# Score maxima in two parts, a batch's logits copied out at once, and unit transposes between the first maxima

## The chip, the cores and the metric

One core of a Trainium2 chip runs the kernel. The metric is the time of one execution in microseconds (us), taken on the device; several executions give a median. The engines are TensorE (PE; its weight loads are PEld), VectorE (DVE), ScalarE (ACT), GpSimd (POOL) and SyncE (SP), which here only issues transfers.

## The reference, cut to what matters

Three stages follow one another; the change touches the first and its hand-over to the second.

```python
def _attn_ref(q, k, v):                      # 4 batches, 8 heads, 1152 rows, 64 columns
    q_pool = q.reshape(B, H, S // 2, 2, D).mean(axis=3)
    scores = scale * np.matmul(q_pool, k.transpose(0, 1, 3, 2))
    scores = scores - np.max(scores, axis=-1, keepdims=True)
    attn = np.exp(scores)
    attn = attn / (np.sum(attn, axis=-1, keepdims=True) + 1e-09)
    return np.matmul(attn, v)

def _moe_ref(x, phi, w1, w2):                # 2304 tokens, 512 wide, 8 experts with 4 slots
    logits = x @ phi
    d = np.exp(logits - logits.max(0, keepdims=True))
    d /= d.sum(0, keepdims=True) + 1e-09
    slot_input = d.T @ x
    ...                                      # an expert's two layers on its slots
    c = np.exp(logits - logits.max(1, keepdims=True))
    c /= c.sum(1, keepdims=True) + 1e-09
    return c @ slot_out
...                                          # then a second, routed mixture of experts
```

## The kernel before

Two heads of one batch form a pair, and there are 16 pairs. A pair is worked off in 18 steps (`NCH`), numbered `s` = 0 to 17, by `step(n)` with `n = 18 * i + s`: the first nine steps take one half of the queries, the other nine the other half, and each step one block of 128 keys. In a step TensorE multiplies queries and keys for both heads (`scores`: lines 374 and 375; the second product adds, as a 65th row, the negated row maximum), and ScalarE takes the exponential out of PSUM (line 376). In step 10 the products with v of the pair's first half follow, 36 matmuls in a row (`weighted`, line 433), and those of its second half in step 1 of the next pair.

The row maxima that `scores` needs have to be known a pair ahead. `s_max(i, j)` computes one of nine blocks of 128 rows: three matmuls of 384 keys each (line 334) into one PSUM tile `s` of three banks, and one VectorE reduction over all 1152 columns (line 343). The pool `ps_s` holds one such tile, so that the next `s_max` starts when that reduction is over. With `apart=True`, used twice at the start, the three parts go into three tiles of the other pool (`new_e`, five banks) and get a reduction each (line 340). `n_group` transposes five or four finished maxima (line 349), ScalarE copies them, and SyncE's queue carries them to the 65th row (line 354).

What else stands in a step is set by tables at the top of the file, from step number to action: `MAXS` (which maximum), `SIDE` (the small groups: q transposes `q0`, `q1`, maxima `n0`, `n1`, row sums `r`, outputs `x0` to `x2`), `BATCH` (m, d, s: the work that follows a batch's last pair, steps above 17 counting into the next pair), `TURN`, `HIGH`, `REST` (transposing and splitting keys of a later pair), `HEADS` (carrying split keys into the tiles `u`, lines 291 and 292), `LOADW` (weights of the second stage), `KLOAD` (keys from HBM, line 246). The first pair has tables of its own (`FIRST`, `FMAX`, `FTURN`). Each engine and each transfer queue works in the order in which the code emits; an instruction that waits holds up all behind it on its engine or queue. All transfers here but the first few stand in SyncE's one queue.

`max_group(b)` transposes a finished batch's logits into a tile of `ps_s`; VectorE takes their maximum, `smax`, from there, and ScalarE then the exponential into `dt`. `d_group` transposes `dt` back, and `sl_group` forms the slot sums. `warm(t, n)` is n transposes of the unit matrix whose results nobody reads.

## Time and profile before

| | |
|---|---|
| median of 3 runs | 701.2 us (697.88 to 702.91) |
| the profiled execution | 700.93 us, of which 698.9 us are the span of the trace |
| instructions | 12442 |
| busy share of the span | PE 94%, PEld 71%, DVE 56%, ACT 49%, POOL 53% |
| mean granted TensorE clock | 0.975 |

The page gives busy times of one execution, a strip of 40 slices of about 17.5 us each, and the chain of work that ended last. The first stage fills the span up to about 510 us, the second up to about 573 us, the rest is the third. In a row of the timeline the first number is the start, the second how long it took (or, with x3, how long three lasted from the first start to the last end), and a bracket at the end says how long the engine stood idle before and what ended that.

### The profile page before, as it was taken

What the parts mean: (1) busy time and instruction counts of PE and PEld (TensorE: products, weight loads), DVE (VectorE), ACT (ScalarE), POOL (GpSimd) and SP (SyncE); (2) the same over time, 40 slices, a digit from 0 to 9 for tenths busy, and PEclk for the clock granted to TensorE, in tenths of its full rate; (3) what the DMA queues carried; (4) which work ended last, traced back from release to release, by engine and by line L of the source; (5) the groups of instructions that cost most, each with busy time, mean ns of one, the idle gap of its engine ahead of it and who ended that gap; (6) DMA issues with size and microseconds to landing.
All of it is one profiled execution on the core that took longest, in us unless ns stands there. A gap on an engine that the chain in (4) does not pass through costs nothing.

```text
span 698.9 us, 12442 instructions
## 1 busy us (share of the span) xinstructions
PE 655.8 (94%) x4330; PEld 495.7 (71%) x4330; DVE 391.9 (56%) x611; ACT 341.7 (49%) x944; POOL 372.4 (53%) x403
## 2 busy tenths in 40 slices
PE   5788999999999999999999999999988989999996
PEld 3655788777687778768778876877753366888885
DVE  5456667667676666767657676764344325522210
ACT  2245566555566556546555654645514046632221
POOL 5454788688777878867678886767700001000000
PEclk9579999999999999999999999999999999999999
DMA  7958778897778978858897895844899924031111
GB/s 135 179 88 177 164 142 215 156 202 198 128 191 165 205 194 150 206 102 214 157 188 189 153 216 92 215 110 106 297 349 385 354 88 155 18 73 46 46 45 48
DMA packets 185090, 114.28 MB, mean 164 GB/s; under 512 B 120888, under 2 KB 158520, under 8 KB 185024
## 3 DMA queue, kind: packets, MB, share of 16 engines
q1 hardware_dynamic: 182976, 112.46, 67.7%
q10 hardware_dynamic: 2048, 0.98, 0.8%
q8 instruction: 36, 0.59, 0.4%
q14 instruction: 30, 0.25, 0.1%
HBM read 66.14 MB, written 4.72 MB: 101 GB/s over the span
## 4 chain that ended last, share of the span: by engine, by line
PE 73%; DVE 8%; DMA 5%; ACT 3%; issue 2%; POOL 1%; SPq 0%; ACTq 0%; POOLq 0%
PE e L433 20%; PE h L1150 14%; PE s L334 11%; PE e L374 8%; PE e L375 7%; DVE nm L343 6%; PE e L469 3%; DMA w<-in_moe_w 2%; DMA en<-in_moe_expert_emb 2%; PE e L410 1%; ACT pt L376 1%; PE e L302 1%; PE h L868 1%; PE h L842 1%; DMA x<-in_moe_w 1%
## 5 line engine op out<-in xcount | busy, mean ns | idle before, releaser
L343 DVE TENSOR_REDUCE nm<-s 128x1 f32<-128x1152 f32 x142 | 192.1, 1353 | 120.1 <-PE s L334 120.0
L376 ACT ACTIVATE pt<-e 128x288 f32<-128x288 f32 x576 | 199.4, 413 | 63.7 <-PE e L375 55.5
L391 POOL TENSOR_TENSOR acc<-acc,pt 128x576 f32<-128x576 f32 x127 | 180.0, 1418 | 15.0 <-ACT pt L376 9.0
L374 PE MATMUL e<-qh,u 128*128 128x288 f32 x576 | 180.1, 328 | 1.2 <-ACT pt L376 1.2
L375 PE MATMUL e<-ql,u 65*128 65x288 f32 x576 | 165.2, 303 | 2.8 <-DMA ql<-nr 2.8
L433 PE MATMUL e<-pt,v 128*64 128x288 f32 x1152 | 149.7, 415 | 0.0
L334 PE MATMUL s<-kh,qb 128*128 128x384 f32 x426 | 109.4, 366 | 15.7 <-DVE nm L343 8.7
L433 PEld LDWEIGHTS e<-pt,v 128*64 128x64 f32 x1152 | 81.0, 139 | 59.6 <-ACT pt L376 5.4
L374 PEld LDWEIGHTS e<-qh,u 128*128 128x128 f32 x576 | 111.9, 194 | 13.6 <-issue 7.6
L375 PEld LDWEIGHTS e<-ql,u 65*128 65x128 f32 x576 | 112.0, 194 | 4.1 <-DMA u<-kh 2.2
L334 PEld LDWEIGHTS s<-kh,qb 128*128 128x128 f32 x426 | 72.1, 197 | 27.9 <-DVE nm L343 17.9
L435 ACT ACTIVATE xu<-e 128x288 f32<-128x288 f32 x32 | 13.1, 410 | 128.5 <-PE e L433 128.5
L389 POOL TENSOR_TENSOR acc<-pt 128x576 f32<-128x576 f32 x32 | 45.4, 1418 | 53.5 <-PE e L418 45.1
L394 DVE TENSOR_REDUCE part<-pt 128x576 f32<-128x1728 f32 x32 | 68.1, 2129 | 0.0
L397 POOL TENSOR_TENSOR acc<-acc,part 128x576 f32<-128x576 f32 x31 | 43.6, 1407 | 36.6 <-DVE part L394 36.5
L1150 PE MATMUL h<-xh,hh 128*128 128x512 f32 x144 | 57.5, 400 | 0.0
L1150 PE MATMUL h<-xh,hl 128*128 128x512 f32 x144 | 57.0, 396 | 0.0
L1150 PE MATMUL h<-xl,hh 128*128 128x512 f32 x144 | 57.0, 396 | 0.0
L285 POOL TENSOR_TENSOR kl<-kl,kh 128x384 fp32r<-128x384 f32 x48 | 48.0, 1001 | 0.6 <-ACT kh L281 0.6
L1127 POOL CAST xh<-x 128x512 fp32r<-128x512 f32 x6 | 3.4, 613 | 63.8 <-PE t L1110 63.8
L1142 DVE SCALAR_TENSOR_TENSOR hl<-c,hh 128x512 fp32r<-128x512 f32 (+1 forms) x22 | 14.0, 642 | 37.8 <-ACT hh L1141 37.8
L469 PE MATMUL e<-ip,xu 128*128 128x192 f32 x160 | 33.9, 328 | 0.0
(232 smaller groups left out, 686.5 us busy)
## 6 DMA issues: line engine op xcount, KB each, us to landing
w<-in_moe_w SPq DMA_DIRECT2D x23, 1024.0 KB
u<-kh SPq DMA_DIRECT2D x96, 192.0 KB
kn<-in_k SPq DMA_DIRECT2D x64, 144.0 KB
u<-kl SPq DMA_DIRECT2D x96, 96.0 KB
v<-in_v SPq DMA_DIRECT2D x32, 288.0 KB
w<-in_moe_w SPq DMA_DIRECT2D x36, 256.0 KB
qh<-hq SPq DMA_DIRECT2D x60, 144.0 KB
qr<-in_q SPq DMA_DIRECT2D x28, 160.0 KB
```

The costliest lines, as they stand in the source:

```text
L285: eng.tensor_tensor(out=t, in0=t.bitcast(F32), in1=hi, op=ALU.subtract)
L334: nc.tensor.matmul(ss[c], qb[j // 6][:, j % 6, :], kh[i % 2][:, c * KC : (c + 1) * KC], start=True, stop=True)
L343: nc.vector.tensor_reduce(out=nm, in_=s[:, :, 0:KC], axis=AX.XY, op=ALU.max, negate=True)
L374: nc.tensor.matmul(e, us[j // 3][:, h, ks], qh[:, h, qs], start=True, stop=False)
L375: nc.tensor.matmul(e, ws[j // 3][:, h, ks], ql[:, h, qs], start=False, stop=True)
L376: nc.scalar.activation(out=pt(n)[:, h, :], in_=e, func=AF.Exp, scale=1.0 / 16.0)
L389: eng.tensor_tensor(out=acc, in0=pt(n - 1), in1=pt(n), op=ALU.add)
L391: eng.tensor_tensor(out=acc, in0=acc, in1=pt(n), op=ALU.add)
L394: nc.vector.tensor_reduce(out=p["part"], in_=pts[n // 3].rearrange("p j h q -> p h q j"), axis=AX.X, op=ALU.add)
L433: nc.tensor.matmul(p["pv"][own[h], 0:HQ], vs[:, h, j, :], pt(n)[:, h, :], start=j == 0, stop=j == J - 1)
L469: nc.tensor.matmul(t[:, n * PW : (n + 1) * PW], xu[:, m * P : (m + 1) * P], ip[:, hp, :], start=True, stop=True)
L1150: nc.tensor.matmul(o, x[:, c, sl], y[:, c, :], start=c + r == 0, stop=c == FC - 1 and r == 2)
```

## The change

- `s_max` without `apart` uses two tiles in place of one: `sa` of two banks for the first two parts and `sb` of one bank for the third, with a reduction each, so that two numbers remain for a block (`nm` becomes 5 x 2). After the last block of a group one more reduction takes the lesser of each two (`nn`), and `n_group` transposes that. With `apart`, the last small step is the lesser of two numbers by `tensor_tensor`.
- `max_group` uses a bank of the five, and ScalarE copies the logits to `dt` at once; maximum and exponential are then taken from `dt`. `sl_group` of the last batch uses `sb`.
- Tables: the maximum of block 3 in step 9 (was 8); m, d, s of a batch at 19, 20, 21 (was 18, 19, 21); the first turned part of the keys in step 0 (was 2), in the first pair one part in step 8 (was 9); the second part of `HEADS` in step 16 (was 15), behind the `KLOAD` of step 15; the first weights of a pair in step 1 (was 3).
- Five groups of unit transposes (24, 6, 12, 16 and 18) stand between and behind the first pair's first five maxima.

```diff
--- before.py
+++ after.py
@@ -32,14 +32,14 @@
 
 
 SIDE = {5: 'q1', 7: 'r', 9: 'x0', 1: 'q0', 13: 'x2', 12: 'n0', 3: 'n1', 14: 'x1'}
-MAXS = {2: 0, 4: 1, 6: 2, 8: 3, 10: 4, 16: 7, 1: 8, 14: 6, 11: 5}
-BATCH = {18: 'm', 19: 'd', 21: 's'}
-
-TURN = {2: 0, 9: 2, 12: 1}
-FTURN = {9: 1, 11: 0, 10: 2}
+MAXS = {2: 0, 4: 1, 6: 2, 10: 4, 16: 7, 1: 8, 14: 6, 11: 5, 9: 3}
+BATCH = {21: 's', 20: 'd', 19: 'm'}
+
+TURN = {9: 2, 12: 1, 0: 0}
+FTURN = {11: 0, 10: 2, 8: 1}
 HIGH = {16: 2, 13: 1, 11: 0}
 REST = {17: 0, 8: 1, 10: 2}
-HEADS = (11, 15, 17)
+HEADS = (11, 16, 17)
 QHEADS = 6
 VISITS = (10, 19)
 
@@ -48,9 +48,11 @@
 FQHEADS = 14
 
 PREAT = 2
-LOADW = (3, 6, 10)
+LOADW = (1, 6, 10)
 QLOAD, KLOAD, VLOAD, QSUM = 5, 15, 6, 12
 FQLOAD, FQSUM = 12, 17
+
+NIDLE = (24, 6, 12, 16, 18)
 
 
 @with_exitstack
@@ -322,31 +324,41 @@
     def s_max(i, j, apart=False):
         p = pairs[i]
         if j in (0, 5):
-            p["nm", j] = sm.tile([P, 5], F32, tag="nm", name="nm", bufs=3)
+            p["nm", j] = sm.tile([P, 5, 2], F32, tag="nm", name="nm", bufs=3)
         j0 = 5 if j > 4 else 0
-        nm = p["nm", j0][:, j - j0 : j - j0 + 1]
+        nm = p["nm", j0][:, j - j0]
+
+        def part(t, c):
+            nc.tensor.matmul(
+                t[:, 0:KC], qb[j // 6][:, j % 6, :], kh[i % 2][:, c * KC : (c + 1) * KC], start=True, stop=True
+            )
+
         if apart:
-            ss = [new_e()[:, 0:KC] for _ in range(3)]
+            ts = [new_e() for _ in range(3)]
+            for c in range(3):
+                part(ts[c], c)
+            n1 = sm.tile([P, 1], F32, tag="n1", name="n1", bufs=2)
+            for t, n in zip(ts, (nm[:, 0:1], nm[:, 1:2], n1)):
+                nc.vector.tensor_reduce(out=n, in_=t[:, 0:KC], axis=AX.X, op=ALU.max, negate=True)
+            nc.vector.tensor_tensor(out=nm[:, 0:1], in0=nm[:, 0:1], in1=n1, op=ALU.min)
         else:
-            s = ps_s.tile([P, 3, 512], F32, tag="s", name="s")
-            ss = [s[:, c, 0:KC] for c in range(3)]
-        for c in range(3):
-            nc.tensor.matmul(
-                ss[c], qb[j // 6][:, j % 6, :], kh[i % 2][:, c * KC : (c + 1) * KC], start=True, stop=True
-            )
-        if apart:
-            n3 = sm.tile([P, 3], F32, tag="n3", name="n3", bufs=2)
-            for c in range(3):
-                nc.vector.tensor_reduce(out=n3[:, c : c + 1], in_=ss[c], axis=AX.X, op=ALU.max, negate=True)
-            nc.vector.tensor_reduce(out=nm, in_=n3, axis=AX.X, op=ALU.min)
-        else:
-            nc.vector.tensor_reduce(out=nm, in_=s[:, :, 0:KC], axis=AX.XY, op=ALU.max, negate=True)
+            s = ps_s.tile([P, 2, 512], F32, tag="sa", name="sa")
+            for c in range(2):
+                part(s[:, c], c)
+            nc.vector.tensor_reduce(out=nm[:, 0:1], in_=s[:, :, 0:KC], axis=AX.XY, op=ALU.max, negate=True)
+            s = ps_s.tile([P, 512], F32, tag="sb", name="sb")
+            part(s, 2)
+            nc.vector.tensor_reduce(out=nm[:, 1:2], in_=s[:, 0:KC], axis=AX.X, op=ALU.max, negate=True)
+        if j in (4, J - 1):
+            n = j - j0 + 1
+            nn = p["nn", j0] = sm.tile([P, 5], F32, tag="nn", name="nn", bufs=3)
+            nc.vector.tensor_reduce(out=nn[:, 0:n], in_=p["nm", j0][:, 0:n], axis=AX.X, op=ALU.min)
 
 
     def n_group(i, part):
         j0, n = (5, J - 5) if part else (0, 5)
         t = new_t()
-        nc.tensor.transpose(t[0:n, 0:P], pairs[i]["nm", j0][:, 0:n], ident)
+        nc.tensor.transpose(t[0:n, 0:P], pairs[i]["nn", j0][:, 0:n], ident)
         nr = sm.tile([5, P], F32R, tag="nr", name="nr", bufs=2)
         nc.scalar.activation(out=nr[0:n], in_=t[0:n, 0:P], func=AF.Copy)
         ql = sets[i % 2][2]
@@ -500,16 +512,18 @@
 
 
     def max_group(b):
-        t = ps_s.tile([P, 3, 512], F32, tag="s", name="s")[:, 0, :]
+        t = new_t()
         nc.tensor.transpose(t[:, 0:P], lk[:, b * JB : (b + 1) * JB, :].rearrange("p m n -> p (m n)"), ident)
         n = P + 64
         nc.tensor.transpose(t[:, P:n], xb[b]["l4"].rearrange("p m n -> p (m n)"), ident[0:64, 0:64])
+
+        dt = xb[b]["dt"] = xp.tile([P, n], F32, tag="dt", name="dt")
+        nc.scalar.activation(out=dt, in_=t[:, 0:n], func=AF.Copy)
         yield
-        nc.vector.tensor_reduce(out=smax[b], in_=t[:, 0:n], axis=AX.X, op=ALU.max, negate=True)
+        nc.vector.tensor_reduce(out=smax[b], in_=dt, axis=AX.X, op=ALU.max, negate=True)
         if b:
             nc.vector.tensor_tensor(out=smax[b], in0=smax[b], in1=smax[b - 1], op=ALU.min)
-        dt = xb[b]["dt"] = xp.tile([P, P + 64], F32, tag="dt", name="dt")
-        nc.scalar.activation(out=dt, in_=t[:, 0 : P + 64], func=AF.Exp, bias=smax[b])
+        nc.scalar.activation(out=dt, in_=dt, func=AF.Exp, bias=smax[b])
         if b:
             cor = xb[b]["cor"] = sm.tile([P, 1], F32, tag="cor", name="cor", bufs=1)
             nc.scalar.activation(out=cor, in_=smax[b - 1], func=AF.Exp, scale=-1.0, bias=smax[b])
@@ -550,7 +564,7 @@
             nc.tensor.matmul(t[ms, cs], d[0:64, 1, ms], xr[:, cs], start=False, stop=True, tile_position=(0, m * NS))
 
     def sl_group(b):
-        t = ps_s.tile([P, 3, 512], F32, tag="s", name="s")[:, 0, :] if b == B - 1 else new_t()
+        t = ps_s.tile([P, 512], F32, tag="sb", name="sb") if b == B - 1 else new_t()
         slot_sums(b, t)
         yield
         if b == B - 1:
@@ -608,16 +622,26 @@
         nc.gpsimd.memset(t[:, PQ:], 0.0)
     nc.gpsimd.memset(ip[:, :, P:PW], 0.0)
     nc.gpsimd.tensor_copy(ip[:, :, 0:P], ident.unsqueeze(1).to_broadcast([P, DC, P]))
+
+    idle = new_e()
+    warm(idle, NIDLE[0])
     s_max(0, 0)
     next(gq[1])
     s_max(0, 1, True)
     run_all(gq[1])
+    idle = new_e()
+    warm(idle, NIDLE[1])
     s_max(0, 2)
+    warm(idle, NIDLE[2])
     s_max(0, 3, True)
     s_max(0, 4)
+    idle = new_e()
+    warm(idle, NIDLE[3])
 
     load_qk(1, "q", nc.scalar)
     run_all(n_group(0, 0))
+    idle = new_e()
+    warm(idle, NIDLE[4])
     by_heads(0, 2)
     load_qk(1, "k")
     load_v(0)
```

## Rows read from the trace of the kernel before

**Rows 1.** The page's strip: granted TensorE clock in tenths, 40 slices.
```profile
PEclk9579999999999999999999999999999999999999
```

**Rows 2.** The page's chain of work that ended last, by line.
```profile
PE e L433 20%; PE h L1150 14%; PE s L334 11%; PE e L374 8%; PE e L375 7%; DVE nm L343 6%; PE e L469 3%; DMA w<-in_moe_w 2%; DMA en<-in_moe_expert_emb 2%; PE e L410 1%; ACT pt L376 1%; PE e L302 1%; PE h L868 1%; PE h L842 1%; DMA x<-in_moe_w 1%
```

**Rows 3.** Windows of two pairs each: length, busy us per engine, clock, DMA.
```profile
93.64:150.95 57.31, 56.66 (x417) 45.21 (x416) 40.17 (x53) 34.18 (x100) 45.52 (x47) 1.00 0.85 183
150.95:210.90 59.95, 58.93 (x435) 45.91 (x434) 41.87 (x60) 34.83 (x102) 46.16 (x45) 1.00 0.79 172
268.40:331.40 63.00, 60.72 (x435) 46.94 (x434) 43.38 (x61) 34.85 (x103) 46.18 (x45) 0.97 0.79 168
```

**Rows 4.** Timeline of TensorE, 99 to 107 us: around three maxima.
```profile
99.34 0.30 PE L375 MATMUL e<-ql,u 65*128 65x288 f32 x1
99.47 0.68 PE L334 MATMUL s<-kh,qb 128*128 128x384 f32 x3
100.00 0.29 PE L374 MATMUL e<-qh,u 128*128 128x288 f32 x1
...
101.04 0.29 PE L375 MATMUL e<-ql,u 65*128 65x288 f32 x1
101.61 0.79 PE L334 MATMUL s<-kh,qb 128*128 128x384 f32 x3 [0.28 <-DVE nm L343]
102.24 0.29 PE L374 MATMUL e<-qh,u 128*128 128x288 f32 x1
...
105.76 0.29 PE L375 MATMUL e<-ql,u 65*128 65x288 f32 x1
...
106.75 0.30 PE L374 MATMUL e<-qh,u 128*128 128x288 f32 x1
```

**Rows 5.** Groups by form on VectorE: busy us, mean ns, idle before.
```profile
L343 DVE TENSOR_REDUCE nm<-s 128x1 f32<-128x1152 f32 x142 | 192.1, 1353 | 120.1 <-PE s L334 120.0
L340 DVE TENSOR_REDUCE n<-e 128x1 f32<-128x384 f32 x6 | 3.0, 549 | 0.0
```

**Rows 6.** One line's instructions on VectorE: ns, min/median/max.
```profile
L510 DVE TENSOR_TENSOR smax<-smax,smax x3: 160/1216/1224, 297.2 to 514.4; 128x1 f32<-128x1 f32 x3
```

**Rows 7.** Timeline of TensorE and VectorE in the first 13 us.
```profile
1.37 3.03 PE L572 MATMUL e<-ident 128*128 128x128 f32 x13 [1.37 <-POOL ident masks.py:199]
8.34 0.90 PE L302 MATMUL e<-ident,qr 128*128 128x128 f32 x3 [3.94 <-DVE qr L259]
...
12.99 1.36 DVE L343 TENSOR_REDUCE nm<-s 128x1 f32<-128x1152 f32 x1 [1.01 <-PE s L334]
```

**Rows 8.** A window at the first stage's end, columns as in rows 3.
```profile
514.00:517.40 3.40, 3.40 (x16) 2.96 (x16) 1.35 (x6) 1.18 (x4) 0.00 (x0) 0.50 1.03 400
```

**Rows 9.** Timeline of SyncE and TensorE, first pair, maxima to the 65th row.
```profile
21.06 1.62 SPq L354 DMA_DIRECT2D ql<-nr  x2
...
37.92 1.36 SPq L354 DMA_DIRECT2D ql<-nr  x2
...
41.63 0.61 PE L375 MATMUL e<-ql,u 65*128 65x288 f32 x1 [0.24 <-DMA ql<-nr]
```

**Rows 10.** Timeline of SyncE, first pair, steps 11 to 17.
```profile
50.52 0.68 SPq L291 DMA_DIRECT2D u<-kh  x1
...
60.28 1.52 SPq L354 DMA_DIRECT2D ql<-nr  x2
```

**Rows 11.** Timeline of SyncE and VectorE: keys from HBM and their use.
```profile
39.38 2.83 SPq L246 DMA_DIRECT2D kn<-in_k  x4
...
46.48 0.58 DVE L278 STREAM_TRANSPOSE kl<-kn 128x384 f32<-128x384 f32 x1 [1.90 <-DMA kn<-in_k]
...
89.89 0.68 SPq L291 DMA_DIRECT2D u<-kh  x1
...
92.67 2.85 SPq L246 DMA_DIRECT2D kn<-in_k  x4
```

**Rows 12.** Timeline of SyncE and the chain, behind the last maxima.
```profile
490.45 26.56 SPq L127 DMA_DIRECT2D w<-in_moe_w  x12
...
545.11 14.40 DMA w<-in_moe_w
```

## The prediction

> **What bounds the kernel now.** I read the page first, then the chain of work that ended last, then windows of the granted clock, then TensorE's timeline pair by pair, and last VectorE's, ScalarE's and SyncE's timelines at the places where TensorE stood.
>
> The chain runs mostly over TensorE, but 6% of the span in it are the maximum reduction of line 343, right behind the 11% of the matmuls of line 334 that feed it [rows 2]. That reduction is not there because VectorE is full: over two ordinary pairs of 57.31 us TensorE is busy for 56.66, VectorE for 40.17, ScalarE for 34.18 [rows 3]. It is there because one tile of three banks serves all maxima, so that TensorE can't begin a block before the reduction of the block before has ended.
>
> What such a wait costs is read from TensorE's timeline [rows 4]. Between the last product of a step (line 375) and the next step's first (line 374) lies one block of maxima. Where it did not wait, the two starts are 99.34 and 100.00, 0.66 apart. At 101.04 and 102.24 they are 1.20 apart, and the block's row names the reduction: a loss of 0.54. At 105.76 and 106.75 they are 0.99 apart: a loss of 0.33. So 0.87 us of a pair of some 28.65 us are lost here, and the same two waits come back in each of the pairs 1 to 14, which compute nine blocks for the pair behind them: 14 x 0.87 = 12.2 us.
>
> Second, the ends of batches. The windows of two pairs around them last 59.95 us for the first batch and 63.00 us for the second (the third is like the second), against 57.31 [rows 3]. The first batch's excess, 2.64, bounds what the batch's own matmuls cost. The other two lose 63.00 - 59.95 = 3.05 us more each, 6.1 in all; their mean clock of 0.97 says that some 3.8 us ran at 1.2 GHz, which alone is 1.9 of the 3.05.
>
> Third, the start. The clock is low in parts of the first three slices [rows 1]. The first slice's digit is not to be trusted: 13 transposes there take 3.03 us, the last one's end included, so some 0.22 each [rows 7], the pace of a window whose clock reads 0.50 (16 transposes in 3.40 us, 0.213 each) [rows 8].
>
> **The change part by part.** The sum is made against the profiled execution, 700.9 us; the median of the runs is 701.2.
>
> *Maxima in two parts.* The trace has no reduction over 768 columns. It lies between 0.549 (384 columns) and 1.353 us (1152) [rows 5]; a straight line through both gives 0.951. Both ends of the wait move: the reduction that frees the next block's first tile starts one matmul earlier (three take 0.68 [rows 4], so about 0.17) and is 1.353 - 0.951 = 0.40 shorter. The tile is free about 0.57 earlier than now. Ahead of the longer wait TensorE stood from about 101.17 (0.13 behind the start at 101.04) to 101.61 [rows 4], that is 0.44. So both waits of a pair should go. The third part has its own bank, free 0.549 after the first reduction, before TensorE comes to it. VectorE pays 0.951 + 0.549 - 1.353 = 0.15 more a block, some 1.4 us a pair, and the small reduction once a group; in 28.65 us it is busy for about 20 [rows 3], so this lies beside TensorE's work. Moving block 3 a step later spreads the blocks and costs nothing by itself. Bounds: 0 (another engine stops TensorE at the same places) to 12.2. The candidate is ScalarE, whose exponentials come two a step; on average it has room (34.18 of 57.31), so I stay near the upper end and take **-11.0**.
>
> *A batch's logits.* They leave the maxima's tile, and ScalarE's copy frees their bank at once, so the maxima no longer wait through reduction, comparison and exponential. But the transposes of `dt` come in step 2, one step after those of the logits, and TensorE works in order: they wait for VectorE's queue (now with the turned keys ahead), for a comparison of two numbers that takes 1.22 us in those two batches and 0.16 us in the last one, where GpSimd is idle [rows 6, 8], and for the exponential. The 36 matmuls of step 1 cover most of that. Bounds 0 to 6.1; I take half, **-3.0**.
>
> The row shows the same instruction at 0.16 us where GpSimd was idle, and at 1.22 us where it was at work. The Trainium skill's "SBUF — State Buffer", section "SBUF: two separate sides", says why: a VectorE instruction with two SBUF inputs and GpSimd exclude each other from one pair of ports for whole instructions. It speaks against the change in one place: the lesser of two numbers with `apart` becomes such an instruction. By it the first maxima could wait for one GpSimd instruction twice more, at most about 2 x 1.06 us by this row, 2.1 us on the sum.
>
> *Unit transposes at the start.* The 24 stand behind the q transposes of 8.34 and ahead of the first maximum, whose reduction now starts at 12.99 [rows 7]. At 0.213 each (16 in 3.40 us) they last from about 8.98 to 14.1; at half that, an estimate for 2.4 GHz, to 11.55. Two matmuls of the first block follow, 0.5 us at full clock and 1.0 at half. So the first reduction starts at 15.1 in the worst case, 2.1 later than now, and in the best case 0.4 earlier, since it waits for two matmuls in place of three and the keys are late anyway. 13 and 16 transposes in rows 7 and 8 kept the slow pace for over 3 us, so I take a rise on the way: 1.0 later. The reductions behind stand back to back on VectorE and grow by three times 0.15 and one small one, 0.5: the first five maxima reach SyncE's queue at 22.6 in place of 21.06 [rows 9].
>
> In the window of rows 8 TensorE did nothing but unit and other transposes at 0.50, and the slot sums behind it ran at full pace, so transposes do raise the clock here. The Trainium skill, "TensorE: Matmul & The Clock Gate", section "Part 4: PE-mode transpose", says that the full clock doesn't engage for transposes. By that rule the 24 all run slowly, the delay is 2.1 in place of 1.0, and the sum comes to 688.7; the trace disagrees.
>
> What the higher clock could give from there to 41 us is not to be had. The second group's maxima go out at 37.92, and TensorE takes them at 41.63 [rows 9]; between 21.06 and 37.92 SyncE's queue issues 20 other transfers back to back and then stands for only some 0.3 us. A faster TensorE waits there for the queue, and idle it loses the clock again. So the delay stays: 1.5 - 0.3 = +1.2. In steps 11 to 17 the dense maxima of the first pair will stop waiting too, but the maxima for pair 1 again stand behind 14 transfers, issued from 50.52 to 60.28 with some 0.5 us of idle time [rows 10]. I count -0.5. Together **+0.7**; bounds -0.7 (best start) and +2.3 (worst start, nothing back).
>
> *Moved transfers.* With `HEADS` at 16, four transfers of split keys (2.6 us) stand behind the load of keys and not ahead of it, so that this load starts at about 89.9 in place of 92.67 [rows 11]. That pays for turning keys in step 0. The weights of step 1 go out while the 36 matmuls run. Zero, with a rival below.
>
> *The end.* `max_group` of the last batch gets one more ScalarE pass, some 0.4 us. TensorE later waits 14.40 us for weights whose loads start at 490.45 [rows 12], when the first stage gives memory back; the pass lies under that. As the loads move with the first stage, what it gains reaches the end. Zero.
>
> Sum: 700.9 - 11.0 - 3.0 + 0.7 = **687.6 us**.
>
> **The rivals.**
>
> *Late keys (slower).* VectorE now turns keys in step 0, ahead of the maximum of step 1, and stands there until the load is in. In the first pair a load issued at 39.38 was used at 46.48 after a wait, 7.1 us [rows 11]. From 89.9 this gives 97.0; the turn, two reductions and the split of q behind it take some 2.5, to 99.5, and TensorE needs the bank that this split frees at about 100.0 [rows 4]. Slack 0.5. Each further microsecond costs one in each of 13 pairs: at 8.6 us after issue the gain is gone, at 9.3 us the loss is 1.7 x 13 = 22, **709.7 us**. For it: transfers fill 0.85 of the time [rows 3]. Against: 7.1 was measured behind a load of v.
>
> *ScalarE takes over (no change by measurement).* Half the waits come back on the exponentials, a batch saves 0.75: 700.9 - 5.5 - 1.5 + 0.7 = **694.6 us**.
>
> *Everything goes (faster still).* Both waits and all of 6.1, the start at its lower bound: 700.9 - 12.2 - 6.1 - 0.7 = **681.9 us**.
>
> *The parts don't free the tile earlier.* If VectorE came late to the first reduction anyway, the two waits of a pair would stay and grow by 0.15 each: 700.9 + 14 x 2 x 0.15 + 0.7 = **705.8 us**. Against it: VectorE idled for 120 us in front of these reductions [rows 5].
>
> **How the numbers follow.** Forecast 0.55 (own range 684 to 692), everything goes 0.15, ScalarE 0.17, no earlier tile 0.05, late keys 0.08. The range 679 to 698 leaves out the last two and the edges of the others, about 0.18. About 1% is what a measurement of this kernel can tell from no change. Faster by over 1%, below 693.9, are the first two and a third of ScalarE's case: 0.75; slower, above 707.9, the late keys: 0.08; the rest, 0.17, lies between.
>
> **What would show it.** Right: two starts around a maximum 0.66 apart throughout, ordinary pairs of some 27.9 us, windows of rows 3 around a batch below 60 us, TensorE waiting at about 36 to 42 us for the maxima's transfer, and the first transfer of maxima after 21.06. Wrong: a wait for `kn` on VectorE in each pair, waits of TensorE for line 376, or full clock from 23 to 50 us with the first 36 matmuls well before 44 us.

## The result and the profile after

| | before | after |
|---|---|---|
| median | 700.62 us (697.88 to 702.91, 4 runs) | 682.9 us (681.85 to 688.36, 4 runs) |
| ratio after/before | | 0.9737 (0.969 to 0.9784) |
| the profiled execution | 700.93 us, span 698.9 | 682.74 us, span 680.7 |
| instructions | 12442 | 12785 |
| mean granted TensorE clock | 0.975 | 0.981 |

687.6 us were forecast, with 679 to 698 as the range. The profiled pair differs by 18.2 us where the sum said 13.3, so the direction and the mechanism can be right and a term is still too small. Which one, the trace only half tells, and the experiments the rest.

The page's strip and chain of work by line, and VectorE's two groups of maxima (busy us, mean ns, idle before), after:

```profile
PEclk9959999999999999999999999999999979999999
PE e L445 20%; PE h L1174 15%; PE e L386 11%; PE e L387 10%; PE sa L332 7%; PE sb L332 3%; PE e L481 3%; DMA w<-in_moe_w 2%; DMA en<-in_moe_expert_emb 2%; DMA ql<-nr 1%; PE e L304 1%; PE e L422 1%; PE h L892 1%; DMA x<-in_moe_w 1%; PE h L866 1%
L348 DVE TENSOR_REDUCE nm<-sa 128x1 f32<-128x768 f32 x142 | 134.7, 948 | 87.3 <-PE sa L332 87.2
L351 DVE TENSOR_REDUCE nm<-sb 128x1 f32<-128x384 f32 x142 | 77.5, 546 | 0.0
```

The 6% of the maximum reduction are gone from the chain [rows 2]; TensorE's lines have taken its place. A reduction over 768 columns takes 0.948 us (0.951 was reckoned from a straight line), and VectorE still idles for 87 us ahead of them. New in this list is the transfer of the maxima, `ql<-nr`, with 1%.

TensorE's timeline of after around two of a pair's maxima, as in [rows 4]:

```profile
128.88 0.30 PE L387 MATMUL e<-ql,u 65*128 65x288 f32 x1
129.02 0.51 PE L332 MATMUL sa<-kh,qb 128*128 128x384 f32 x2
129.37 0.33 PE L332 MATMUL sb<-kh,qb 128*128 128x384 f32 x1
129.54 0.29 PE L386 MATMUL e<-qh,u 128*128 128x288 f32 x1
...
130.58 0.29 PE L387 MATMUL e<-ql,u 65*128 65x288 f32 x1
130.71 0.51 PE L332 MATMUL sa<-kh,qb 128*128 128x384 f32 x2
131.06 0.42 PE L332 MATMUL sb<-kh,qb 128*128 128x384 f32 x1
131.32 0.29 PE L386 MATMUL e<-qh,u 128*128 128x288 f32 x1
```

From the last product of a step to the next step's first it is 0.66 us in the first case and 0.74 in the second, where before had 1.20 there. From pair 1 on no maxima's matmul waits for its tile; each starts 0.13 to 0.19 us behind the product ahead of it, most of them 0.13 or 0.14.

Windows of after (columns as in [rows 3]): two ordinary pairs, the second of them alone, two pairs around the first batch's end and two around the second's:

```profile
94.55:150.86 56.31, 55.93 (x415) 44.91 (x415) 42.05 (x75) 33.94 (x100) 45.61 (x46) 1.00 0.78 185
123.17:150.86 27.69, 27.69 (x208) 22.39 (x208) 20.04 (x38) 16.91 (x50) 22.21 (x23) 1.00 0.75 183
150.86:208.21 57.35, 57.35 (x436) 45.55 (x435) 43.67 (x82) 34.70 (x103) 46.17 (x46) 1.00 0.77 184
264.80:322.45 57.65, 57.65 (x436) 45.68 (x435) 44.03 (x83) 34.63 (x104) 46.17 (x45) 1.00 0.78 182
```

In an undisturbed pair TensorE is now busy throughout (27.69 of 27.69). The pair ahead of it is 0.9 us longer, around a wait for a transfer of maxima. Around a batch TensorE no longer stands and the clock no longer falls: 57.35 and 57.65 in place of 59.95 and 63.00. Against two undisturbed pairs (55.38) a batch costs 2.0 to 2.3 us more, where before it cost 2.64 and 5.69 more than its ordinary ones.

The start, SyncE's and TensorE's timelines of after, which answer [rows 9, 10]:

```profile
20.88 1.62 SPq L366 DMA_DIRECT2D ql<-nr  x2
...
37.50 1.43 SPq L366 DMA_DIRECT2D ql<-nr  x2
...
60.86 1.53 SPq L366 DMA_DIRECT2D ql<-nr  x2
```

```profile
41.20 0.61 PE L387 MATMUL e<-ql,u 65*128 65x288 f32 x1 [3.85 <-DMA kn<-in_k]
...
62.80 0.40 PE L387 MATMUL e<-ql,u 65*128 65x288 f32 x1 [1.53 <-DMA ql<-nr]
```

Windows of after at the start, columns as above:

```profile
8.00:34.30 26.30, 22.47 (x147) 19.44 (x146) 16.50 (x32) 10.22 (x29) 15.99 (x42) 1.00 0.74 164
30.00:32.00 2.00, 0.94 (x7) 0.52 (x5) 1.95 (x6) 0.40 (x1) 1.96 (x2) 1.00 0.95 215
34.30:48.00 13.70, 8.87 (x33) 5.75 (x33) 5.66 (x7) 4.15 (x11) 3.61 (x4) 0.50 0.56 106
37.30:41.20 3.90, 0.06 (x1) 0.00 (x0) 1.00 (x2) 0.00 (x0) 0.00 (x0) 0.50 1.05 206
```

With the unit transposes TensorE stays at 2.4 GHz until 34.30. And yet the second group of maxima leaves at 37.50, where it left at 37.92: TensorE runs out of work from 30 us on, is at 1.2 GHz from 34.30, and then stands for 3.85 us. (The row names the load of keys as what ended that wait; the product reads the 65th row, whose transfer was issued at 37.50, and e6 and e10 below show that it is this transfer.) Pair 1 is reached (its products with v in step 1) at 65.38, against 65.02 before.

Cut at these products, the 18.3 us between the profiles lie as follows: +0.36 up to there; -13.6 in the six pairs around the three batches; -5.1 in the other pairs from 1 on (of which -2.3 in one pair, where before waited 0.63 for a transfer of maxima and 0.51 for an exponential); nothing behind the first stage, whose gain reaches the end whole.

### The profile page after: what moved, and what is told of

The parts are those of the page before. It is cut to its first block, busy times and chain, and to the rows that moved or that the text cites. A ratio compares the mean times of both kernels' runs of the same rounds, so it can differ in the third digit from the quotient of the medians.

```text
span 680.7 us, 12785 instructions
## 1 busy us (share of the span) xinstructions
PE 649.6 (95%) x4406; PEld 496.5 (73%) x4406; DVE 404.1 (59%) x785; ACT 339.8 (50%) x948; POOL 372.8 (55%) x403
## 4 chain that ended last, share of the span: by engine, by line
PE 80%; DMA 6%; DVE 2%; ACT 1%; SPq 1%; issue 1%; POOL 1%; ACTq 0%; POOLq 0%
PE e L445 20%; PE h L1174 15%; PE e L386 11%; PE e L387 10%; PE sa L332 7%; PE sb L332 3%; PE e L481 3%; DMA w<-in_moe_w 2%; DMA en<-in_moe_expert_emb 2%; DMA ql<-nr 1%; PE e L304 1%; PE e L422 1%; PE h L892 1%; DMA x<-in_moe_w 1%; PE h L866 1%
## 5 line engine op out<-in xcount | busy, mean ns | idle before, releaser
L388 ACT ACTIVATE pt<-e 128x288 f32<-128x288 f32 x576 | 196.1, 413 | 56.5 <-PE e L387 47.4
L348 DVE TENSOR_REDUCE nm<-sa 128x1 f32<-128x768 f32 x142 | 134.7, 948 | 87.3 <-PE sa L332 87.2
L386 PE MATMUL e<-qh,u 128*128 128x288 f32 x576 | 177.4, 325 | 1.4 <-ACT pt L388 1.1
L387 PE MATMUL e<-ql,u 65*128 65x288 f32 x576 | 162.9, 299 | 6.9 <-DMA kn<-in_k 3.8
L386 PEld LDWEIGHTS e<-qh,u 128*128 128x128 f32 x576 | 109.8, 191 | 13.5 <-issue 7.6
L387 PEld LDWEIGHTS e<-ql,u 65*128 65x128 f32 x576 | 110.1, 191 | 8.8 <-DMA ql<-nr 8.0
L351 DVE TENSOR_REDUCE nm<-sb 128x1 f32<-128x384 f32 x142 | 77.5, 546 | 0.0
L332 PE MATMUL sa<-kh,qb 128*128 128x384 f32 x284 | 74.5, 344 | 3.1 <-DVE nm L348 2.1
L409 POOL TENSOR_TENSOR acc<-acc,part 128x576 f32<-128x576 f32 x31 | 43.7, 1411 | 37.5 <-DVE part L406 35.8
L332 PE MATMUL sb<-kh,qb 128*128 128x384 f32 x142 | 50.9, 359 | 0.0
L332 PEld LDWEIGHTS sa<-kh,qb 128*128 128x128 f32 x284 | 46.2, 192 | 5.0 <-DVE nm L348 3.6
```

What stands on the lines that cost most here:

```text
L332: nc.tensor.matmul(t[:, 0:KC], qb[j // 6][:, j % 6, :], kh[i % 2][:, c * KC : (c + 1) * KC], start=True, stop=True)
L348: nc.vector.tensor_reduce(out=nm[:, 0:1], in_=s[:, :, 0:KC], axis=AX.XY, op=ALU.max, negate=True)
L351: nc.vector.tensor_reduce(out=nm[:, 1:2], in_=s[:, 0:KC], axis=AX.X, op=ALU.max, negate=True)
L386: nc.tensor.matmul(e, us[j // 3][:, h, ks], qh[:, h, qs], start=True, stop=False)
L387: nc.tensor.matmul(e, ws[j // 3][:, h, ks], ql[:, h, qs], start=False, stop=True)
L388: nc.scalar.activation(out=pt(n)[:, h, :], in_=e, func=AF.Exp, scale=1.0 / 16.0)
```

## The experiments

Two questions stood open. What of the gain is the maxima's, what the batch's, what the tables'? And what bounds the start: the clock, which the unit transposes are there for, or SyncE's queue? Those runs that have the changed kernel as their base are measured against the kernel before like the change itself; the change as it is was run once more among them (e5), as their yardstick.

**No unit transposes (e1).**

```diff
-NIDLE = (24, 6, 12, 16, 18)
+NIDLE = (0, 0, 0, 0, 0)
```

> The changed kernel without its five groups of unit transposes (24, 6, 12, 16, 18 set to 0). Theory (the first pair hangs on SyncE's queue, which starts with the first group of maxima at about 21 us and lets TensorE into step 9 only at about 41 us, whatever its clock was before): 681 to 684 us, within 1.5 us of the changed kernel's 682.9, with the first 36 matmuls again at 43.5 to 45 us. Rival (the transposes' clock is worth what it looks like, 13 us at 2.4 in place of 1.2 GHz while TensorE works through steps 0 to 8): 686 to 690 us, the first 36 matmuls at 47 us or later.

Measured: 679.04 us, ratio 0.9703 (0.9659 to 0.9747), a little below the 681 to 684 expected; the first 36 matmuls begin at 43.19. Windows of e1:

```profile
8.00:16.00 8.00, 5.80 (x16) 4.21 (x16) 6.18 (x14) 3.68 (x9) 6.82 (x31) 0.57 0.61 148
18.70:28.90 10.20, 7.80 (x27) 7.07 (x28) 3.37 (x7) 3.56 (x9) 2.55 (x2) 0.50 0.79 154
35.80:46.00 10.20, 7.32 (x26) 5.13 (x28) 3.63 (x5) 3.79 (x10) 1.52 (x2) 0.50 0.65 120
```

TensorE runs at 1.2 GHz over most of the first 46 us (from 28.9 to 35.8 at 2.4), and nothing is lost: the maxima leave at 19.93, 0.95 earlier than in after, and pair 1 is reached at 64.39. The clock isn't what sets the start.

**The change unaltered (e5).**

> The changed kernel once more, unaltered, beside the next three on the same chip, to see whether the unit transposes cost what the kernel without them suggested (679.0 against 682.9, taken at two different times). If they do, its ratio to the kernel before lies again near 0.974 (682 to 684 us at 701 before), clear of the 0.970 without them; if the difference was the chip's, near 0.970 (680 us).

Measured: 681.77 us, 0.9708 (0.9667 to 0.9749). That is e1's ratio to 0.0005; the unit transposes are worth nothing that can be measured, in either direction (each ratio is known to about 0.004, some 3 us). What e1 lay below its expectation was thus not the transposes'. Both ratios of the change, 0.9737 and 0.9708, go into the comparisons below; their mean is 0.972.

**Twice the first unit transposes (e8).**

```diff
-NIDLE = (24, 6, 12, 16, 18)
+NIDLE = (48, 6, 12, 16, 18)
```

> The changed kernel with 48 unit transposes in place of 24 ahead of the first maximum: 24 more at 0.107 to 0.213 us each hold the first maxima back by 2.6 to 5.1 us. Theory (the first pair is a chain from the first maxima over SyncE's queue to step 9 and on, and nothing behind it has room): the first transfer of maxima at 23.4 to 25 us and 2.5 to 4 us on the time, 685 to 687 us. Rival (the first pair has room behind the first maxima, so that their delay is taken up): 682 to 684 us.

Measured: 682.83 us, 0.9714 (0.9663 to 0.9765), 1.06 above e5, with intervals that overlap; the 685 to 687 of the theory were missed, and the time is that of the rival. The trace shows the delay itself, on TensorE and on SyncE:

```profile
24.22 1.62 SPq L366 DMA_DIRECT2D ql<-nr  x2
```

The maxima leave 2.65 us later than in e5 (21.57), the products of step 10 begin 2.0 later (47.09 against 45.09) and those of pair 1 3.6 later (68.53 against 64.93). So a late first maximum does go through to pair 1. Between the two profiled executions it stays to the end (spans of 682.8 and 678.5), but that of e8 is the slowest of its four and that of e5 the fastest of its six; between the medians it does not. How much of such a delay the whole run keeps stays open.

**The second group of maxima on another queue (e6).** Without unit transposes, ScalarE issues the maxima of the first pair's second half and of pair 1's first.

```diff
+        queue = nc.scalar if 2 * i + part in (1, 2) else nc.sync
-            nc.sync.dma_start(
+            queue.dma_start(
```

> The changed kernel without unit transposes and with two transfers moved: the maxima of the first pair's second group and of pair 1's first group go out on ScalarE's queue in place of SyncE's, where 20 and 14 transfers stand ahead of them. Theory (these queues hold TensorE at step 9 and at step 18, and its idling there costs it the clock): the first 36 matmuls begin at 37 to 40 us in place of 43.2, step 18 is reached 4 to 7 us earlier, and the time is 672 to 676 us. Rival (another thing, the keys or the halves of q, holds the first pair at the same place): 678 to 680 us, as without the move.

Measured: 675.68 us, 0.9621 (0.958 to 0.9662). ScalarE's and TensorE's timelines of e6:

```profile
33.95 1.88 ACTq L367 DMA_DIRECT2D ql<-nr  x2
35.88 0.52 ACT L283 ACTIVATE kh<-kl 128x384 fp32r<-128x384 f32 x1 [1.96 <-issue]
```

```profile
37.91 1.01 PE L332 MATMUL sa<-kh,qb 128*128 128x384 f32 x2 [2.42 <-ACT qb L308]
```

The transfer goes out 3.5 us earlier than in after, but ScalarE stands 1.96 us to issue it, the copy of q behind it is late, and TensorE waits 2.42 for that. So the products of step 10 came at 42.05 and not at 37 to 40 as expected; pair 1 came at 61.43, 4 us earlier than in after. The time is as expected, the way to it only in part.

**Later loads in the queue (e10).** The same without ScalarE's cost in step 7: the transfers of `phi` and of v for pair 1 go behind the maxima (step 8), and only pair 1's first maxima are issued by ScalarE. No unit transposes.

```diff
-    for h in range(2):
-        nc.sync.dma_start(... phi ...)
-    load_v(1)
...
+            if n == 8:
+                for h in range(2):
+                    nc.sync.dma_start(... phi ...)
+                load_v(1)
...
+        queue = nc.scalar if (i, part) == (1, 0) else nc.sync
```

> The changed kernel without unit transposes, with the loads of phi and of pair 1's v moved from ahead of the loop into step 8 (four transfers, 2.6 us of SyncE's issuing, no longer ahead of the first pair's second maxima, which go out on SyncE's queue again), and pair 1's first maxima on ScalarE's queue. Theory (SyncE's queue holds step 9, and moving the maxima to ScalarE's queue cost ScalarE 2 us of issuing in step 7): the second maxima go out at about 34 in place of 37.5 us, the first 36 matmuls begin at 39 to 41 us, and the time is 672 to 676 us, the same or 1 to 3 us less than with both on ScalarE's queue (675.7). Rival (v or phi is then late for pair 1): 678 us or more.

Measured: 674.78 us, 0.9631 (0.9594 to 0.9668). SyncE's and TensorE's timelines of e10:

```profile
34.60 1.32 SPq L367 DMA_DIRECT2D ql<-nr  x2
```

```profile
40.64 4.87 PE L446 MATMUL e<-pt,v 128*64 128x288 f32 x36
```

Four transfers out of the way, and the maxima leave 2.9 us earlier, step 10's products begin 3.5 earlier and pair 1 4.9 earlier (60.52) than in after. That is the queue as the bound of the start, shown from two sides (e6, e10) with one result. Both beat the changed kernel by about 1% (0.9621 and 0.9631 against 0.972; against e1, which like them has no unit transposes, by 0.7 to 0.8%) and the kernel before by almost 4%. Both also moved pair 1's first maxima; the share of each move wasn't measured.

**One tile for the maxima again (e3).** The changed kernel, but `s_max`, `n_group` and the last `sl_group` as in before.

```diff
-            s = ps_s.tile([P, 2, 512], F32, tag="sa", name="sa")
...
+            s = ps_s.tile([P, 3, 512], F32, tag="s", name="s")
...
+            nc.vector.tensor_reduce(out=nm, in_=s[:, :, 0:KC], axis=AX.XY, op=ALU.max, negate=True)
```

> The changed kernel with the maxima as before: one tile of three banks, one reduction over 1152 columns; all else as changed (batch part, tables, unit transposes). Theory (the wait for that one tile costs 0.87 us a pair and some more with the tables as they are now): 692 to 695 us, 9 to 12 us more than the changed kernel, and waits for the reduction at TensorE in each pair. Rival (the moved steps alone take those waits away): 682 to 686 us.

Measured: 695.84 us, 0.9933 (0.9902 to 0.9964), just above the 692 to 695 expected. The maxima in two parts are worth 0.9933 - 0.972 = 0.021 of 701 us, some 15 us, when all else is there (12 between the profiled executions). TensorE's timeline of e3 at two of a pair's maxima:

```profile
131.46 0.29 PE L377 MATMUL e<-ql,u 65*128 65x288 f32 x1
132.03 0.79 PE L336 MATMUL s<-kh,qb 128*128 128x384 f32 x3 [0.28 <-DVE nm L345]
132.65 0.30 PE L376 MATMUL e<-qh,u 128*128 128x288 f32 x1
...
138.42 0.29 PE L377 MATMUL e<-ql,u 65*128 65x288 f32 x1
138.98 0.79 PE L336 MATMUL s<-kh,qb 128*128 128x384 f32 x3 [0.26 <-DVE nm L345]
```

The two waits of [rows 4] are back, as distances of 0.57 and 0.56 us from the product ahead to the maximum (0.13 without a wait). The second one is longer than in before: with block 3 in step 9, its reduction is over later.

**The tables alone (e4).** Before with `MAXS`, `TURN`, `FTURN`, `HEADS` and `LOADW` of after, all else as it was.

```diff
-MAXS = {2: 0, 4: 1, 6: 2, 8: 3, 10: 4, 16: 7, 1: 8, 14: 6, 11: 5}
+MAXS = {2: 0, 4: 1, 6: 2, 10: 4, 16: 7, 1: 8, 14: 6, 11: 5, 9: 3}
...
-TURN = {2: 0, 9: 2, 12: 1}
+TURN = {9: 2, 12: 1, 0: 0}
...
```

> The kernel before with only the moved steps of the change (block 3 in step 9, turned keys in step 0 and 8, split keys in step 16, weights in step 1), no other part. Theory (the moves make room and are worth nothing themselves; at most the later block 3 takes one of the two waits of a pair, 0.33 us x 14): 696 to 702 us. Rival (the moves carry the gain of the ordinary pairs): 688 to 692 us.

Measured: 703.0 us, 1.0034 (1.0006 to 1.0063), 2.4 us slower than before (0.4 to 4.4 by the interval) and 1 us above the range expected. Two ordinary pairs of e4:

```profile
95.75:153.47 57.72, 56.65 (x416) 45.17 (x415) 40.27 (x53) 34.02 (x100) 45.56 (x47) 1.00 0.84 182
```

0.41 more for two pairs than in before [rows 3]. The second of a pair's two waits is longer: 0.55 us from the product ahead to the maximum, where before has 0.35. 14 pairs of half of 0.41 are 2.9 us, about the loss measured. By itself the move of block 3 costs; with two parts the wait that it lengthens isn't there.

**The old batch part (e2).** The changed kernel, but the logits stay in PSUM, in the third part's bank, through maximum and exponential, with m and d at 18 and 19.

```diff
-BATCH = {21: 's', 20: 'd', 19: 'm'}
+BATCH = {18: 'm', 19: 'd', 21: 's'}
...
-        nc.scalar.activation(out=dt, in_=t[:, 0:n], func=AF.Copy)
```

> The changed kernel with the batch part undone: logits transposed into the tile of the third part (sb), maximum and exponential taken from PSUM, m and d of a batch at 18 and 19 as before. Theory from the two traces (two pairs around a batch got 0.9, 3.65 and 3.8 us shorter beyond the ordinary pairs' gain): 690 to 692 us, 7 to 9 us more than the changed kernel, with the clock falling at the second and third batch. Rival (the forecast's half, -3.0, and the rest of those windows is the maxima's doing): 685 to 687 us.

Measured: 684.4 us, 0.9765 (0.9728 to 0.9801). This was a miss: 690 to 692 were expected, since the batch windows had shrunk by so much more than the ordinary ones. Against the change's 0.972 it is 0.0045 of 701 us, 3 us, with intervals that overlap. The traces say the same more firmly: the six pairs around the three batches' ends take 175.8 us in e2 and 172.4 to 172.8 in after, e1, e5 and e8, which all have the new batch part.

**The maxima alone (e9).** Before with only `s_max`, `n_group` and `sl_group` of after, and the old batch part in the third part's bank.

```diff
+            s = ps_s.tile([P, 2, 512], F32, tag="sa", name="sa")
...
+            s = ps_s.tile([P, 512], F32, tag="sb", name="sb")
...
-        t = ps_s.tile([P, 3, 512], F32, tag="s", name="s")[:, 0, :]
+        t = ps_s.tile([P, 512], F32, tag="sb", name="sb")
```

> The kernel before with only the maxima in two parts (and their banks); tables, batch order and start as before, a batch's logits in the third part's bank. The forecast gave the maxima -11.0 us whether the tables move or not; the kernel with all but the maxima changed still had ordinary pairs of 28.83 us, and that with the tables alone 28.85, against 27.67 at best in the changed kernel. Theory (the parts carry nearly all, the tables only make room): ordinary pairs of 27.7 to 27.9 us and 684 to 688 us. Rival (parts and moved block 3 need one another): ordinary pairs of 28.2 us or more and 691 to 696 us.

Measured: 687.38 us, 0.98 (0.9742 to 0.9857), 14 us (10 to 18 by the interval) of the change's 20 or so without any other part of it. The time is the theory's. But four of the ordinary pairs take 28.1 to 28.2 us and not 27.7 to 27.9; in three of these TensorE waits for a transfer of maxima.

With e2, e3, e4 and e9 the second batch's end is known for each way to combine the two parts. The window of two pairs around it, of e2, e3, e4 and e9 in this order:

```profile
265.96:324.78 58.82, 58.34 (x435) 45.66 (x434) 44.42 (x83) 34.52 (x103) 46.30 (x46) 1.00 0.77 180
```

```profile
270.12:330.03 59.91, 58.75 (x435) 45.89 (x434) 43.26 (x61) 34.78 (x104) 46.19 (x45) 1.00 0.82 175
```

```profile
271.52:333.46 61.94, 59.15 (x435) 45.91 (x434) 43.53 (x61) 34.68 (x103) 46.27 (x45) 1.00 0.79 170
```

```profile
264.81:324.57 59.76, 58.41 (x436) 45.51 (x435) 44.84 (x83) 34.82 (x103) 45.81 (x45) 1.00 0.75 176
```

Less two ordinary pairs of the same kernel (55.45 in e2, 57.65 in e3 and 57.72 in e4 by the same view, two undisturbed pairs of 27.69 for after and e9), the batch's excess is as follows. (e2 and e3 differ from e9 and e4 also in the start, which lies far ahead.)

| | old batch part, old tables | old batch part, moved steps | new batch part, moved steps |
|---|---|---|---|
| one tile | 5.69 (before) | 4.22 (e4) | 2.26 (e3) |
| two parts | 4.38 (e9) | 3.37 (e2) | 2.27 (after) |

Each part alone takes away some of the excess. With the moved steps in place the new batch part is worth 2.0 us at this batch with one tile (4.22 to 2.26) and 1.1 on top of two parts; the two parts are worth 0.9 to 1.3 with the old batch part and nothing with the new one. Of the 5.69 in before some goes with the clock, which fell there (0.97) and not in e4's execution (1.00). The moved steps take part too: in e9 the comparison of two numbers takes 1.29 us at the second batch and 1.26 at the third, in e2 0.23 and 0.25. Held in the third part's bank, the logits stop only one matmul of the next maximum and no longer all three; the third batch in e9, on TensorE:

```profile
410.37 0.44 PE L330 MATMUL sb<-kh,qb 128*128 128x384 f32 x1 [1.18 <-ACT dt L522]
```

It is the matmul into `sb` that waits for the exponential, with the two into `sa` ahead of it done. What the windows showed is the sum of all three, and I had put it down to one.

**Keys two steps later (e7).**

```diff
-QLOAD, KLOAD, VLOAD, QSUM = 5, 15, 6, 12
+QLOAD, KLOAD, VLOAD, QSUM = 5, 17, 6, 12
```

> The changed kernel with the load of keys issued in step 17, behind the last split keys, in place of step 15: some 5.3 us later. It measures the forecast's rival of late keys. In the changed kernel VectorE stands 1.5 us on average for keys in step 0 and ends the split of q some 2.3 to 2.9 us before TensorE needs its bank. By the rival's mechanism the keys come 2.4 to 3 us too late in each of 13 pairs: 31 to 39 us more, 714 to 722 us, with TensorE waiting behind VectorE at steps 2 or 3. If VectorE's stand in step 0 were harmless in any case: 682 to 685 us.

Measured: 753.95 us, 1.0727 (1.0653 to 1.08), over 30 us more than expected. The waits of VectorE on the keys in after, then in e7 (us in total, times, longest), and VectorE's and TensorE's timelines of e7:

```profile
DVE kl L280 <- DMA kn<-in_k: 19.2, 13, 5.9
```

```profile
DVE kl L280 <- DMA kn<-in_k: 95.5, 15, 9.1
```

```profile
172.34 0.58 DVE L280 STREAM_TRANSPOSE kl<-kn 128x384 f32<-128x384 f32 x1 [6.26 <-DMA kn<-in_k]
...
173.91 0.59 PE L332 MATMUL sa<-kh,qb 128*128 128x384 f32 x2 [2.78 <-DVE nm L348]
```

The turn of the keys holds up VectorE's queue for 6.26 us, the maximum behind it is late, and TensorE stands 2.78 us ahead of the next maximum. Each of the 13 pairs has such a wait, of 1.9 to 3.7 us, 37 us in all. The pairs grew by some 5.5 us ((753.95 - 681.77) / 13), twice the wait at that place. Two windows of e7 from a pair's products of step 1 to those of step 10 tell where the rest comes from; in after this takes 14.60 (123.17 to 137.77):

```profile
131.06:152.06 21.00, 17.87 (x115) 14.30 (x114) 10.29 (x21) 9.78 (x27) 11.92 (x11) 0.84 0.60 137
165.13:183.01 17.88, 15.10 (x114) 11.57 (x113) 10.10 (x21) 9.29 (x27) 11.94 (x11) 1.00 0.60 136
```

In the second window, where the clock holds, the wait costs 3.28. In the first, where it falls behind a wait of 3.13 (mean 0.84), as it does in several pairs, the same work takes 6.40 more.

## Why the prediction was right, and what was mis-sized

**The maxima's tile: right.** The mechanism is as told: with a tile of two banks and one of one, no maximum waits any more. The new reduction was reckoned to 3 ns. Both waits went, so the full 0.87 a pair was saved, and a bit more: an undisturbed pair is 27.69 against 28.65, 0.96 less. ScalarE, whose rival was given 0.17, takes nothing over (TensorE waits 1.1 us for exponentials at L386 in all, 1.2 before). Of the 13.4 us that 14 pairs would make, some came back at once: in pairs 1, 2 and 6 TensorE waits for a transfer of maxima; those pairs are 0.9 to 1.5 us longer (in pair 1 by the lower clock behind the wait). The term as a whole, -11.0, was somewhat too small: alone it measured -14 (e9; the interval of 10 to 18 us still holds 11), 12.7 from pair 1 on between the profiled executions. What it left out is the batches' ends, where two parts also shorten the old wait: 7.4 of the 12.7 lie in the six pairs there, for which the sum had six times 0.79, 4.7. On top of the rest it measured -15 (e3), 12 between the profiles.

**A batch's logits: the size is right, the account of the batches' ends is not.** -3.0 was forecast and, on top of two parts, 3 us was measured (e2). Yet the windows around batches shrank by far more: of the 18.3 us of the profiles 13.6 lie there, where the sum had put 3.0 and six times 0.79, 7.7 in all. Put in one after the other, the two parts take 7.4 us off these six pairs (before to e9), the moved steps 2.9 (e9 to e2) and the batch part 3.2 (e2 to after). So the batch part is as reckoned, the two parts gave 2.7 more, and the moved steps, set at nothing, gave 2.9. About 2 of these 2.9 are the two comparisons: in e9 the maximum's matmul waits 1.2 us behind each, in e2 0.2 at most. (One execution each; in another order the shares would differ, as the table of excesses shows.) Two steps of the prediction failed: the bound of 6.1, which took the batch's loss as the batch part's alone and the ordinary waits as all that the two parts could save, and the zero for the moved steps. The fear that `dt`'s transposes would wait in step 2 was idle; TensorE was busy in all of the 57.65 us of that window.

The row of 1.22 us [rows 6] told of a comparison that met GpSimd at work. In after the same one took 0.159 to 0.282 us, the two comparisons at the start 0.159 and 0.190, with GpSimd no less busy (46 of 57.6 us). In before the one at 297.18 ended at 298.40, with GpSimd's addition (298.38); in after the second batch's began 0.2 us after such an addition was over, and the third's met the last 0.27 us of one and ended with it (410.30 and 410.29). The Trainium skill, "SBUF — State Buffer", section "SBUF: two separate sides", says that such an instruction and one of GpSimd that reads SBUF exclude each other; by it I had bounded a loss of 2.1 us, and none came. The runs at the batches agree with the rule (in e9 the mean of the three is 0.906 us again): whether two instructions meet depends on when they come, and these hardly did. The one of 0.190 at the start had a GpSimd instruction beside it by the profile, whose spans of GpSimd are rough, and didn't wait.

**The start: right, by the queue.** +0.7 was forecast, and pair 1 came 0.36 later, although q came 1 us earlier in that execution (its transposes at 7.36 against 8.34). In e5, the same kernel, it came at 64.93, 0.09 earlier than in before; so the size of this term isn't settled by single executions. The first maxima left at 20.88 (21.57 in e5) and not at 22.6: the sign "after 21.06" failed in the one and held in the other. TensorE waits at 37 to 41 us, as told, the clock falls as told (a little ahead of that wait, when work runs short), and e1, e6 and e10 show from three sides that SyncE's queue sets this stretch. On the clock, two windows of after, of which the first holds only transposes on TensorE and the second the last of the unit transposes and the first maximum, and two of e2, whose record of the clock begins earlier, with TensorE still at its 24 unit transposes:

```profile
8.05:10.40 2.35, 2.35 (x13) 2.35 (x13) 1.28 (x3) 2.28 (x6) 1.72 (x3) 1.00 0.25 54
10.40:12.00 1.60, 1.60 (x15) 1.60 (x15) 0.19 (x1) 0.42 (x2) 1.51 (x2) 1.00 0.53 122
```

```profile
10.00:11.00 1.00, 1.00 (x7) 1.00 (x5) 0.56 (x1) 0.87 (x3) 0.77 (x2) 0.50 0.82 191
11.00:12.00 1.00, 1.00 (x9) 1.00 (x8) 0.00 (x0) 0.00 (x0) 1.00 (x2) 0.72 0.41 97
```

In after 13 take 2.35 us, 0.18 each; the next 15 take 1.60, 0.11 each, half of the 0.213 of [rows 8]. (The clock of 1.00 in the first window isn't to be trusted, as in the page's first slice; the pace is.) In e2 the granted clock itself rises, from 0.50 in the first window to 0.72 as the mean of the second and 1.00 behind it. Transposes in fp32 bring TensorE to 2.4 GHz here. The Trainium skill, "TensorE: Matmul & The Clock Gate", section "Part 4: PE-mode transpose", says that the full clock doesn't engage for transposes in TensorE's transpose mode. The rows show these as matmuls and don't say in which mode they run; for them the measurement decides. For the time of the start the clock decides nothing (e1).

**The moved transfers: right, with more room than reckoned.** The load of keys starts at 90.92 (89.9 was reckoned), but its keys are in 5.3 us after issue (a later pair's, 118.84 to 124.11) and not 7.1. In after VectorE waits for keys 13 times, 19.2 us in all. The prediction had named such a wait in each pair as a sign of being wrong; it came in nearly each, and TensorE doesn't wait behind it. VectorE's timeline of after:

```profile
124.11 0.58 DVE L280 STREAM_TRANSPOSE kl<-kn 128x384 f32<-128x384 f32 x1 [0.94 <-DMA kn<-in_k]
124.61 0.92 DVE L348 TENSOR_REDUCE nm<-sa 128x1 f32<-128x768 f32 x1
```

The reduction behind the turn is over at 125.53, 3.49 us ahead of the next maximum at 129.02, and the split of q at 126.67; a slack of 0.5 had been reckoned. The rival was real as a mechanism, but its place was another and its price too low. In e7 the turn comes 6.27 us later behind a pair's products than in after (7.21 against 0.94), 2.78 beyond those 3.49: just the wait of TensorE there, at the next maximum for the reduction, and not at the bank that the split of q frees. One for one, as the prediction had it, the waits of the 13 pairs make 37 us; 72 were lost, in part since TensorE's clock falls behind such waits.

**No reduction over earlier tiles, and everything goes.** The rival in which the parts free nothing earlier fell with the first two distances of 0.66 and 0.74. The one in which everything goes, 681.9, is nearest to the measured time, with 0.15, but that is in part luck: the batch part gave some 3 of its 6.1 and the start none of its -0.7, while the moved steps gave what stood in no sum. The moved steps, block 3's among them, cost 2.4 us by themselves (e4); with the two parts no cost shows (e2, which has them, 0.9765; e9, which hasn't, 0.98).

## What to carry to other kernels

A PSUM tile that is computed and reduced as a whole makes its writer wait for the reader's whole pass; two tiles with a reduction each cost VectorE 0.14 us a block here and take the wait away. Where several edits relieve the same stall, bound what they save by the stall itself, not by a share for each, and undo each alone before one is given the credit. Before a warm-up of the clock is put into a chain, look for the queue that the chain ends in: here four transfers put behind it and one given to another queue were worth about 1%, and the clock nothing that could be measured.

## What the runs showed of the hardware

- Unit transposes in fp32 raise TensorE to 2.4 GHz (e2: granted clock 0.50 from 10 to 11 us, 1.00 from 12 us); in after, once TensorE has run short of work from 30 us on, it is back at 1.2 from 34.3 to 48.0. With and without the transposes the time is the same (0.9708 and 0.9703).
- A VectorE comparison of two numbers in SBUF takes 0.16 us alone; beside an addition of GpSimd it lasted until that was over (1.22 us in before, 1.26 and 1.29 in e9).
- Issuing two small transfers takes ScalarE 1.96 us (e6) in which it computes nothing; SyncE takes 1.3 to 1.6 us for the like.
- A wait of TensorE of some 3 us in each pair cost 5.5 us a pair on average: 3.3 in a pair where the clock holds, 6.4 in one where it falls behind the wait (e7).
